# GpSimd joins the halves of w1's pieces for their sums, in place of TensorE's identity products

## The chip, the cores and the metric

One core of a Trainium2 chip runs the whole program. The metric is the device time of one launch in microseconds (us), of which several runs are made; a profile of one execution is read beside it. TensorE (PE) multiplies, VectorE (DVE), ScalarE (ACT) and GpSimd (POOL) work on vectors, and SyncE (SP) issues all DMAs here.

## What is computed

The attention works in chunks of 64 tokens, a gated layer (d_ff 2048) follows, then a second layer with a softmax-weighted unit and a normalization (d_ff 1024). There are 4608 tokens of width 512.

```python
scores = scale * np.matmul(q_c, k_c.transpose(0, 1, 2, 4, 3))
...
out = np.matmul(attn, v_c)

h = x @ w_in
g = h * (1.0 / (1.0 + np.exp(-h)))
return (g @ w_out).astype(np.float32)

h = x @ w_in
...
solu = h * sm
...
return (ln @ w_out).astype(np.float32)
```

## The kernel before

Every operand of a product is held as two float16 halves, high and low (`split`, L107: ACT writes the high half, VectorE or GpSimd the low one), and a product is three matmuls: high by high, high by low, low by high. The tokens go in nine blocks of 512. In blocks 0 and 1 (`FAST = 2`) the products with w1 and w2 are plain: `h_group` (L357) makes one of 16 columns groups of h by 12 matmuls, `x_part` (L637) gathers g @ w2. From block 2 on both are done on quarters with seven products in place of eight, and for that the weights must be there as sums and differences of their quarters. These are made once, while blocks 1 and 2 run, are written to DRAM (`w1s`, `w2s`), and are read back through a ring of tiles (`Ring`, L447).

The weights arrive as 64-bit numbers. `dec_scale`, `dec_bits` and `dec_split` (L124 to L150) decode a piece: ACT scales (L129), VectorE shifts and joins bits (L136, L137, L139), then ACT and GpSimd, or for w4 ACT and VectorE, split it. The last pieces, w3 and w4, are decoded in block 1; from the 33rd piece on the intermediate `wy` lies in SBUF, before in a PSUM bank (`wp`). w3's low halves are GpSimd's (L114, `w3q`), w4's VectorE's (L115, `w4l`).

The sums of w1 are the place of the change. w1 has eight pairs of pieces: piece p holds the upper rows of two column groups p and p + 8. `w1_sums(p)` (L422) stands in the loop over f of block 1 at the steps of the table `W1F` (L66). It calls `sums` (L408), which stores three quarters as they are (L411) and calls `pe_sums` (L380). There the high and low halves of each quarter are added in PSUM by two products with an identity (L391, tile `wq`, two banks a piece), ACT copies two quarters out (L398, `y`), and VectorE makes four sums (L403 to L406). Then each of four results is split again (L110 on ACT, L114 on GpSimd, tile `ws`, three staging buffers `xb0` to `xb2`) and stored (L417).

Beside it in block 1 run four `m_h` (L658, at f = 5, 7, 9, 11): two banks of products with w3 (L664), and for each the chain `m_norm` (L740) over VectorE, ACT and GpSimd: maximum (L670), exponential (L764), product with the sum (L766), square (L772), power on GpSimd (L779), scaling (L782), split (L783, L784) and two transposing DMAs (L794). One buffer each for `e` and `u` makes the four chains follow each other. `m_out` (L807, at f = 13, 15 and behind the loop) needs the transposed `uT` and all of w4. All PSUM tiles come from one pool of eight banks (`ps1`, L77), so TensorE waits where a bank is still read.

The order on each engine is found by the Tile scheduler from the program's order and priorities; `w1_sums` stands under `tc.high_priority(offset=1)`.

```python
with tc.high_priority(offset=1):
    for p in range(8):
        if W1F[p] == f:
            w1_sums(p)
```

Of the kernel before, what the change touches and what calls it, by code (L numbers as in the profile page):

```python
# [8 lines left out]
F32 = mybir.dt.float32  # L9
F16 = mybir.dt.float16  # L10
I32 = mybir.dt.int32
AF = mybir.ActivationFunctionType
ALU = mybir.AluOpType
# [3 lines left out]
P = 128  # L17
# [9 lines left out]
K1 = F1 // P  # L27
# [19 lines left out]
def fused(ctx: ExitStack, tc: tile.TileContext, qkv, w1, w2, w3, w4, g_ln, out):  # L47
    nc = tc.nc
    V, A, G, T = nc.vector, nc.scalar, nc.gpsimd, nc.tensor
# [14 lines left out]
    MO = (0, 1, 2, 3)  # L64
    W3S = [0, 3]
    W1F = [3, 5, 7, 9, 11, 13, 14, 15]  # L66
    W2F = [3, 1, 7, 3]
    EXB = [6, 7, 10, 13, 14]
    PHA = [4, 5, 6, 7, 8, 10, 11, 15, 32, 33, 34, 35]
# [4 lines left out]
    one = ctx.enter_context(tc.tile_pool(name="one", bufs=1))  # L74
# [7 lines left out]
    w1t = [one.tile([P, 2, KD, P], F16, tag=f"w1_{f}", name=f"w1_{f}") for f in range(K1)]  # L82
    w2t = {}
    for d in range(KD):
        for f in range(4):
            if f % 2 == 0:
                tag = f"w2_{2 * d + f // 2}" if d < 3 else f"q{12 + f // 2}"
                y = one.tile([P, 2, 2, 4, P], F16, tag=tag, name="w2t")
                w2t[d, f], w2t[d, f + 1] = y[:, 0], y[:, 1]

    w1s = [dram.tile([7, P, 2, 2, 2, P], F16, name=f"w1s{i}") for i in range(4)]
# [15 lines left out]
    def split(dst_h, dst_l, src, scale, eng_h, eng_l):  # L107

        if eng_h is A:
            A.activation(dst_h, src, AF.Copy, scale=scale)  # L110
        else:
            V.tensor_scalar(out=dst_h, in0=src, scalar1=scale, scalar2=None, op0=ALU.mult)
        if eng_l is G and scale == 1.0:
            return G.tensor_tensor(out=dst_l, in0=src, in1=dst_h, op=ALU.subtract).ins  # L114
        return V.scalar_tensor_tensor(out=dst_l, in0=src, scalar=scale, in1=dst_h,  # L115
                                      op0=ALU.mult, op1=ALU.subtract).ins
# [202 lines left out]
    xb, xf = {}, {}  # L319
# [54 lines left out]
    def flat(a, keep):  # L374

        if len(a.shape) == keep + 1:
            return a
        return a.rearrange("p l a b -> p l (a b)" if keep == 2 else "p a b -> p (a b)")

    def pe_sums(ys, quads, y1122=None):  # L380

        ys, quads = ([flat(a, k) for a in v] for v, k in ((ys, 1), (quads, 2)))
        n = 512 // quads[0].shape[2]

        def whole(qs):
            ps = [bank([P, n, 512 // n], "wq") for _ in range(len(qs) // n)]
            out = []
            for i, a in enumerate(qs):
                o = ps[i // n][:, i % n]
                for l in range(2):  # L390
                    T.matmul(o, ident16, a[:, l], start=l == 0, stop=l == 1)  # L391
                out.append(o)
            return ps, out

        y11, y12, y21, y22 = ys
        ps, o = whole([quads[0], quads[3]])
        if n == 2:
            A.activation(y1122, ps[0], AF.Copy)  # L398
        else:
            A.activation(y11, o[0], AF.Copy)  # L400
            A.activation(y22, o[1], AF.Copy)
        _, (p21, p12) = whole([quads[2], quads[1]])
        V.tensor_tensor(out=y22, in0=p21, in1=y22, op=ALU.add)  # L403
        V.tensor_tensor(out=y21, in0=y11, in1=p21, op=ALU.subtract)
        V.tensor_tensor(out=y11, in0=y22, in1=y11, op=ALU.subtract)
        V.tensor_tensor(out=y12, in0=p12, in1=y11, op=ALU.subtract)  # L406

    def sums(quads, dst, ys, staging, y1122=None):  # L408
        with tc.issue_after(last[0]):
            for j, a in ((0, quads[0]), (4, quads[1]), (6, quads[3])):  # L410
                nc.sync.dma_start(out=dst(j), in_=a)  # L411
        pe_sums(ys, quads, y1122)
        y11, y12, y21, y22 = ys
        for y, j in ((y11, 1), (y22, 2), (y21, 3), (y12, 5)):
            z = staging()
            split(z[:, 0], z[:, 1], y, 1.0, A, G)
            nc.sync.dma_start(out=dst(j), in_=z)  # L417

    sn, last = [0], [None]
    UL = V  # L420

    def w1_sums(p):  # L422
        wa, wb = w1t[p], w1t[p + K1 // 2]
        y = one.tile([P, 4, 2, P], F32, tag=f"q{10 + p % 2}", name="y")

        def staging():
            sn[0] += 1
            return one.tile([P, 2, 2, P], F16, tag=f"xb{sn[0] % 3}", name="ws")

        sums((wa[:, :, 0:2], wa[:, :, 2:4], wb[:, :, 0:2], wb[:, :, 2:4]),  # L430
             lambda j: w1s[p // 2][j, :, p % 2], [y[:, i] for i in range(4)], staging,
             y[:, 0::3].rearrange("p n a b -> p n (a b)"))

    def w2_sums(c, q):
        ys = [one.tile([P, 2, 4, P], F32, tag=f"q{10 + i}", name="y") for i in range(2)]
# [44 lines left out]
    def bank(shape, name):  # L480
        return ps1.tile(shape, F32, tag="mm", name=name)
# [361 lines left out]
    for k in range(KD):  # L843
        for n in range(2):
            y = w3q[n, k // 2]
# [43 lines left out]
    def weights(n=1):  # L889
        for _ in range(n):  # L890
            d3()
            d1()
            d2()
# [36 lines left out]
    for b in range(NB):  # L930
        m = b * TPB + TPB
        more = b + 1 < NB
        if FAST <= b:
            q_alloc(b)
        for f in range(K1):
            if b < FAST:
                if b == 1 and f in MHF:
                    n = MHF.index(f)
                    run(m_h(b - 1, MO[n], "m1", ("m2", ("h4", "h5"), ("h6", "h7"), ("h2", "h3"))[n]))
                if b == 1 and f in MOF:  # L940
                    run(m_out(b - 1, MO[MOF.index(f)]))
                h_group(b, f)
                if b == 0:
                    weights(NW0[f])
                    if f:
                        g_split(b, f - 1, GH)
                else:
                    y = g_split(b, f, A)
                    with tc.high_priority(offset=-50):
                        weights(NW1[f])  # L950
                    with tc.high_priority(offset=1):
                        for p in range(8):
                            if W1F[p] == f:
                                w1_sums(p)
                    if f == QF:
                        load_qk(m, ("q8",))
                        prep_qk(m, ahead=False)
            elif f % 8 == 0:
                if f and more:
                    load_qk(m, ("w1_14", "w1_15"))  # L960
                    prep_qk(m, ahead=False)
                if b == FAST:
                    for n in range(2):
                        run(m_h(b - 1, MO[f // 4 + n], *(("m1", "m2"), ("w2_5", "w2_4"))[n % 2]))
                if f and b == FAST:
                    for n in range(2):
                        run(m_out(b - 1, MO[n]))
                elif b > FAST:
                    run(m_fast(b - 1, 1) if f else begun, in_turn(*(m_out(b - 1, MO[n]) for n in range(2) if f)))
                run(h_fast(b, f // 4), h_fast(b, f // 4 + 1))  # L970
        if b == 0:
            g_split(b, K1 - 1, GH)
        else:
            run(m_out(b - 1, MO[TPB - 2], low=more))
        if b == FAST - 1:
            ring.load()
        def step(s):

            if not more:
                return  # L980
            if s == 0:
                if b < FAST - 1:
                    load_qk(m)
                    prep_qk(m)
                else:
                    load_qk(after(m))
                prep_v(m)
            if b and s == 1:
                run(m_out(b - 1, MO[TPB - 1]))
            AT_P = (3, 4, 6, 7) if b == 0 else (3, 4, 5, 6)  # L990
            if s in AT_S:
                i = AT_S.index(s)
                n = m + ORDER[i]
                a_scores(n)
                if i < 3:
                    prep_qk(m + ORDER[i + 1], V if b == 1 else G)
                a_norm(n, eng_l=V if b else G)
            if s in AT_P:
                i = AT_P.index(s)
                a_pv(m + ORDER[i])  # L1000
            if b == 0:
                with tc.high_priority(offset=-50):
                    weights(NX[s])
            if b == FAST and s in W3S:
                w3_sums(W3S.index(s))
            if b == 1:
                weights(NX1[s])
            for n in range(4):
                if b == 1 and W2F[n] == s:
                    w2_sums(n // 2, n % 2)  # L1010

        if b < FAST:
            for s in range(8):
                step(s)
                x_part(b, s // 2, s % 2)
        else:
            begun = m_fast(b, 0, alt=not more)
            x_fast(b, step, begun)

    b = NB - 1  # L1020
# [52 lines left out]
```

## Time and profile before

| | us |
|---|---|
| runs of the kernel, median of 3 | 1179.76 |
| lowest, highest run | 1178.94, 1181.08 |
| profiled execution, first to last instruction | 1179.4 |
| TensorE busy in it | 1127.8 (96%) |
| VectorE busy | 911.7 (77%) |
| GpSimd busy | 249.1 (21%) |

The page gives no other time for the profiled execution than its span; it lies 0.4 us under the median of the runs. Matmuls are pipelined, so their durations overlap: the pace is read from one start to the next. The granted TensorE clock (PEclk) is a share of the full 2.4 GHz, 0.50 is 1.2 GHz. "Idle before" names what ended an engine's wait. Line numbers are those of the kernel before; in the changed kernel they are up to 18 higher.

### The profile page before, as it was taken

The page shows a single profiled execution, that of the slowest core. Times are in us where ns is not written, and L with a number is a line of the kernel's source. Part 1 is how long each engine was busy: PE and PEld are TensorE (multiplying, and loading weights), DVE is VectorE, ACT ScalarE, POOL GpSimd, SP SyncE. Part 2 cuts the span into 40 slices and gives each one's busy share as a digit, 9 for nine tenths or more (in the row PEclk, how much of TensorE's full clock was granted, in tenths as well). Part 3 has the DMA queues.
Part 4 walks back from the last instruction along what each step waited for, and adds up shares of the span by engine and source line. Part 5 has one row for each costly group of instructions (what it writes and reads, how often), then busy time and mean ns, then how long its engine had stood idle before and what let it go on. Part 6 is the DMA issues. An engine that isn't in the chain of part 4 may idle for free.

```text
span 1179.4 us, 23566 instructions
## 1 busy us (share of the span) xinstructions
PE 1127.8 (96%) x9036; PEld 769.1 (65%) x9036; DVE 911.7 (77%) x1638; ACT 802.8 (68%) x1475; POOL 249.1 (21%) x243
## 2 busy tenths in 40 slices
PE   5999998998999999999999999999999999999998
PEld 4444443444657875887678767876787677777853
DVE  5999998487578787888778877888689868886453
ACT  6886678676667777856785677568756876577253
POOL 3655433334101510021003100310031002100001
PEclk9999899999999999999999999999999999999999
DMA  7667488543536564776577657666776676665704
GB/s 259 225 190 206 155 233 268 165 135 112 139 113 203 165 189 133 204 204 202 143 192 213 196 151 188 204 198 155 182 211 198 161 180 197 179 161 137 210 21 116
DMA packets 205169, 209.18 MB, mean 177 GB/s; under 512 B 120192, under 2 KB 130432, under 8 KB 205056
## 3 DMA queue, kind: packets, MB, share of 16 engines
q1 hardware_dynamic: 205056, 207.68, 61.5%
q8 instruction: 70, 1.15, 0.4%
q14 instruction: 43, 0.35, 0.1%
HBM read 156.24 MB, written 24.12 MB: 153 GB/s over the span
## 4 chain that ended last, share of the span: by engine, by line
PE 59%; DVE 16%; ACT 10%; DMA 7%; issue 6%; POOL 2%; SPq 0%; ACTq 0%; POOLq 0%; DVEq 0%
PE o_ps L821 5%; PE o_ps L813 5%; PE o_ps L814 5%; PE pa L491 3%; PE pa L594 3%; PE pa L592 3%; PE pa L593 3%; PE pa L493 3%; PE pa L492 3%; DVE vbl L115 2%; PE pa L708 2%; PE pa L709 2%; PE pa L710 2%; PE pb L491 2%; PE pb L493 2%
## 5 line engine op out<-in xcount | busy, mean ns | idle before, releaser
L110 ACT ACTIVATE q<-hc 128x512 f16<-128x512 f32 x196 | 119.1, 624 | 41.4 <-DVE hc L579 16.4
L115 DVE SCALAR_TENSOR_TENSOR q<-hc,q 128x512 f16<-128x512 f32 x196 | 138.0, 719 | 6.9 <-ACT q L110 5.5
L114 POOL TENSOR_TENSOR qbl<-qk,qbh 64x512 f16<-64x512 f32 x54 | 71.0, 1314 | 266.2 <-ACT qbh L110 223.6
L593 PE MATMUL pa<-q,ring 128*128 128x256 f16 x448 | 122.1, 273 | 0.0
L592 PE MATMUL pa<-q,ring 128*128 128x256 f16 x448 | 122.1, 273 | 0.0
L594 PE MATMUL pa<-q,ring 128*128 128x256 f16 x448 | 122.1, 273 | 0.0
L813 PE MATMUL o_ps<-w4h,uT 128*128 128x512 f16 x288 | 109.1, 379 | 0.4 <-DVE e L766 0.4
L814 PE MATMUL o_ps<-w4l,uT 128*128 128x512 f16 x288 | 109.2, 379 | 0.0
L779 POOL TENSOR_TENSOR c<-c,mhalf 128x2 f32<-128x2 f32 (+1 forms) x22 | 14.1, 640 | 392.1 <-DVE c L778 382.2
L492 PEld LDWEIGHTS <-ring 128*128 128x128 f16 x784 | 77.0, 98 | 18.4 <-issue 7.9
L491 PEld LDWEIGHTS <-ring 128*128 128x128 f16 x784 | 77.0, 98 | 11.5 <-DMA ring<-w1s 0.8
L592 PEld LDWEIGHTS <-ring 128*128 128x128 f16 x784 | 76.7, 98 | 11.1
L593 PEld LDWEIGHTS <-ring 128*128 128x128 f16 x784 | 76.7, 98 | 11.0
L493 PEld LDWEIGHTS <-ring 128*128 128x128 f16 x784 | 77.0, 98 | 9.2
L594 PEld LDWEIGHTS <-ring 128*128 128x128 f16 x784 | 76.7, 98 | 8.9
L821 PE MATMUL o_ps<-w4h,uT 128*128 128x512 f16 x288 | 70.2, 379 | 0.0
L491 PE MATMUL pa<-x,ring 128*128 128x256 f16 x224 | 61.6, 275 | 6.7 <-ACT hc L513 4.3
L493 PE MATMUL pa<-x,ring 128*128 128x256 f16 x224 | 61.7, 275 | 0.0
L492 PE MATMUL pa<-x,ring 128*128 128x256 f16 x224 | 61.6, 275 | 0.0
L491 PE MATMUL pb<-x,ring 128*128 128x256 f16 x224 | 61.1, 273 | 0.6 <-DMA ring<-w1s 0.6
L592 PE MATMUL pb<-q,ring 128*128 128x256 f16 x224 | 61.1, 273 | 0.0
L593 PE MATMUL pb<-q,ring 128*128 128x256 f16 x224 | 61.1, 273 | 0.0
(277 smaller groups left out, 3486.4 us busy)
## 6 DMA issues: line engine op xcount, KB each, us to landing
ring<-w1s SPq DMA_DIRECT2D x196, 256.0 KB, 3.4
ring<-w2s SPq DMA_DIRECT2D x196, 256.0 KB, 3.8
wst<-w SPq DMA_DIRECT2D x48, 512.0 KB, 4.1
qk<-qkv SPq DMA_DIRECT2D x29, 512.0 KB, 3.8
vs<-qkv SPq DMA_DIRECT2D x36, 256.0 KB, 3.2
out<-o SPq DMA_DIRECT2D x36, 256.0 KB, 2.2
w1s<-ws SPq DMA_DIRECT2D x32, 128.0 KB, 2.1
w2s<-ws SPq DMA_DIRECT2D x16, 256.0 KB, 2.0
```

The lines of the kernel that those rows point to most:

```text
L110: A.activation(dst_h, src, AF.Copy, scale=scale)
L114: return G.tensor_tensor(out=dst_l, in0=src, in1=dst_h, op=ALU.subtract).ins
L115: return V.scalar_tensor_tensor(out=dst_l, in0=src, scalar=scale, in1=dst_h, op0=ALU.mult, op1=ALU.subtract).ins
L491: T.matmul(ps[:, c], wh, x[:, 0, k], start=first, stop=False, skip_group_check=True)
L492: T.matmul(ps[:, c], wh, x[:, 1, k], start=False, stop=False, skip_group_check=True)
L493: T.matmul(ps[:, c], wl, x[:, 0, k], start=False, stop=k == 1, skip_group_check=True)
L592: T.matmul(ps[:, c], wh, g[:, 0], start=first, stop=False, skip_group_check=True)
L593: T.matmul(ps[:, c], wh, g[:, 1], start=False, stop=False, skip_group_check=True)
L594: T.matmul(ps[:, c], wl, g[:, 0], start=False, stop=q == 1 and f == 3, skip_group_check=True)
L813: T.matmul(ps, uh[:, k], w4h[:, k, :], start=k == 0, stop=False)
L814: T.matmul(ps, uh[:, k], w4l[:, k, :], start=False, stop=False)
L821: T.matmul(ps, ul[:, k], w4h[:, k, :], start=False, stop=k == K2 - 1)
```

## The change

The halves of each w1 piece are no longer added by identity products. A new function `join` adds them on GpSimd, two instructions of 512 elements a piece, into the tile `y` that the sums use (`w1_join`, at steps of a new table `W1J`). The sums (`quad_sums`) read only that tile. The four results are then split two at a time: two ACT and two GpSimd instructions of 512 in place of four each of 256, in a staging tile twice as large, from which the same four stores are made.

```diff
+    W1J = [1, 3, 5, 7, 9, 11, 13, 14]
...
-    def pe_sums(ys, quads, y1122=None):
+    def pe_sums(ys, quads):
...
-        if n == 2:
-            A.activation(y1122, ps[0], AF.Copy)
-        else:
-            A.activation(y11, o[0], AF.Copy)
-            A.activation(y22, o[1], AF.Copy)
+        A.activation(y11, o[0], AF.Copy)
+        A.activation(y22, o[1], AF.Copy)
...
+    def quad_sums(ys):
+        y11, y12, y21, y22 = ys
+        V.tensor_tensor(out=y22, in0=y21, in1=y22, op=ALU.add)
+        V.tensor_tensor(out=y21, in0=y11, in1=y21, op=ALU.subtract)
+        V.tensor_tensor(out=y11, in0=y22, in1=y11, op=ALU.subtract)
+        V.tensor_tensor(out=y12, in0=y12, in1=y11, op=ALU.subtract)
+
+    def join(y, w):
+        G.tensor_tensor(out=y, in0=flat(w[:, 0], 1), in1=flat(w[:, 1], 1), op=ALU.add)
...
+    def w1_join(p):
+        y1[p] = y = one.tile([P, 4, 2 * P], F32, tag=f"q{10 + p % 2}", name="y")
+        for i in range(2):
+            join(y[:, 2 * i:2 * i + 2].rearrange("p n a -> p (n a)"), w1t[p + i * K1 // 2])
+
     def w1_sums(p):
         wa, wb = w1t[p], w1t[p + K1 // 2]
-        y = one.tile([P, 4, 2, P], F32, tag=f"q{10 + p % 2}", name="y")
-
-        def staging():
+        y = y1.pop(p)
+        dst = lambda j: w1s[p // 2][j, :, p % 2].rearrange("p l a b -> p l (a b)")
+        with tc.issue_after(last[0]):
+            for j, a in ((0, wa[:, :, 0:2]), (4, wa[:, :, 2:4]), (6, wb[:, :, 2:4])):
+                nc.sync.dma_start(out=w1s[p // 2][j, :, p % 2], in_=a)
+        quad_sums([y[:, i] for i in range(4)])
+        for i, js in ((0, (1, 5)), (2, (3, 2))):
             sn[0] += 1
-            return one.tile([P, 2, 2, P], F16, tag=f"xb{sn[0] % 3}", name="ws")
-
-        sums((wa[:, :, 0:2], wa[:, :, 2:4], wb[:, :, 0:2], wb[:, :, 2:4]),
-             lambda j: w1s[p // 2][j, :, p % 2], [y[:, i] for i in range(4)], staging,
-             y[:, 0::3].rearrange("p n a b -> p n (a b)"))
+            z = one.tile([P, 2, 2, 2 * P], F16, tag=f"xb{sn[0] % 3}", name="ws")
+            split(z[:, 0], z[:, 1], y[:, i:i + 2], 1.0, A, G)
+            for k in range(2):
+                nc.sync.dma_start(out=dst(js[k]), in_=z[:, :, k])
...
                             if W1F[p] == f:
                                 w1_sums(p)
+                            if W1J[p] == f:
+                                w1_join(p)
```

The scheduler puts the work in another order. GpSimd's queue from the splits of w3 on, before (`w3q` is w3, `ws` a staging tile of sums, `c` the power of an m_norm):

```order
L114 TENSOR_TENSOR w3q<-wy,w3q 128x512 x8
L114 TENSOR_TENSOR ws<-y,ws 128x256 x4
L779 TENSOR_TENSOR c<-c,mhalf 128x1
L114 TENSOR_TENSOR ws<-y,ws 128x256 x5
L779 TENSOR_TENSOR c<-c,mhalf 128x1
```

and changed (`y<-w` is a join):

```order
L115 TENSOR_TENSOR w3q<-wy,w3q 128x512 x2
L414 TENSOR_TENSOR y<-w_0_72 128x512
L414 TENSOR_TENSOR y<-w_8_80 128x512
L115 TENSOR_TENSOR w3q<-wy,w3q 128x512
L414 TENSOR_TENSOR y<-w_1_73 128x512
L414 TENSOR_TENSOR y<-w_9_81 128x512
L115 TENSOR_TENSOR w3q<-wy,w3q 128x512
L115 TENSOR_TENSOR ws<-y,ws 128x512 x2
L414 TENSOR_TENSOR y<-w_2_74 128x512
L115 TENSOR_TENSOR w3q<-wy,w3q 128x512
```

Joins and splits of the first pieces now stand among the eight splits of w3; six joins and four `ws` splits come before or between them and the last one.

VectorE's queue from the end of m_norm 1 (`u_1931`) to the second product of m_norm 2 (`e_2072`), before; `y_2129` is piece 3 of w1, `w4l` the last piece of w4:

```order
L784 TENSOR_TENSOR u_1931<-e_1925,u_1931 128x1024
L672 TENSOR_REDUCE mm__2076<-mp_2073 128x1
L115 SCALAR_TENSOR_TENSOR w4l_109<-wy_2041,gs_110,w4h_108 128x512
L761 TENSOR_SCALAR nm_2079<-mm__2076 128x1
L115 SCALAR_TENSOR_TENSOR g_2036<-g_2120,g_2036 128x512
L403 TENSOR_TENSOR y_2129<-wq_2139,y_2129 128x256
L404 TENSOR_TENSOR y_2129<-y_2129,wq_2139 128x256
L405 TENSOR_TENSOR y_2129<-y_2129 128x256
L406 TENSOR_TENSOR y_2129<-wq_2139,y_2129 128x256
L115 SCALAR_TENSOR_TENSOR g_2179<-g_2177,g_2179 128x512
L766 SCALAR_TENSOR_TENSOR e_2072,us_2086<-h2_ps_2046,u_2078 128x512
```

and the end of the same stretch changed (`y_2305` is piece 6, `y_2343` piece 7, `e_2030` m_norm 2's `e`, L784 the former L766):

```order
L408 TENSOR_TENSOR y_2305<-y_2305 128x256
L116 SCALAR_TENSOR_TENSOR w4l_109<-wy_1999,gs_110,w4h_108 128x512
L409 TENSOR_TENSOR y_2305<-y_2305 128x256
L408 TENSOR_TENSOR y_2343<-y_2343 128x256
L410 TENSOR_TENSOR y_2305<-y_2305 128x256
L409 TENSOR_TENSOR y_2343<-y_2343 128x256
L411 TENSOR_TENSOR y_2305<-y_2305 128x256
L784 SCALAR_TENSOR_TENSOR e_2030,us_2044<-h2_ps_2004,u_2036 128x512
```

The sums have moved up by three to four pieces: where those of piece 3 stood, those of pieces 6 and 7 stand, and the last `w4l`, which stood two rows behind the end of m_norm 1 (counted from 0), has a sum of piece 6 ahead of it.

## Rows read from the trace of the kernel before

**Rows 1.** The page, busy us, share of the span and instructions by engine.

```profile
PE 1127.8 (96%) x9036; PEld 769.1 (65%) x9036; DVE 911.7 (77%) x1638; ACT 802.8 (68%) x1475; POOL 249.1 (21%) x243
```

**Rows 2.** Busy time by stretch: PE, PEld, DVE, ACT, POOL, then PEclk, DMA, GB/s.

```profile
131.20:160.00 28.80, 28.80 (x143) 13.89 (x142) 28.23 (x43) 20.20 (x35) 9.54 (x8) 1.00 0.57 171
160.00:197.00 37.00, 30.51 (x149) 14.37 (x148) 33.94 (x70) 32.25 (x59) 14.71 (x15) 1.00 0.92 264
197.00:225.00 28.00, 27.57 (x160) 13.88 (x159) 16.75 (x44) 19.97 (x39) 8.53 (x13) 1.00 0.63 195
...
236.00:242.00 6.00, 4.43 (x34) 2.59 (x35) 3.70 (x7) 4.03 (x7) 0.35 (x1) 0.72 0.38 112
```

**Rows 3.** TensorE's waits from 131 to 242: total us, times, longest.

```profile
PE wq L391 <- DVE e L766: 2.9, 1, 2.9
PE h_ps L362 <- DVE y L406: 2.1, 1, 2.1
PE s_ps L211 <- ACT kb L110: 1.4, 1, 1.4
...
PE s_ps L212 <- DVE kb L115: 0.6, 1, 0.6
```

**Rows 4.** Timeline of VectorE, 180 to 210: start, us, line, operation, out<-in.

```profile
180.50 0.68 DVE L766 SCALAR_TENSOR_TENSOR e<-h_ps,u 128x512 f32<-128x512 f32 x1
...
188.12 1.69 DVE L784 TENSOR_TENSOR u<-e,u 128x1024 f16<-128x1024 f32 x1
...
197.24 0.68 DVE L766 SCALAR_TENSOR_TENSOR e<-h_ps,u 128x512 f32<-128x512 f32 x1
...
209.56 0.68 DVE L766 SCALAR_TENSOR_TENSOR e<-h_ps,u 128x512 f32<-128x512 f32 x1
```

**Rows 5.** Timeline of TensorE, first identity products.

```profile
141.55 0.71 PE L391 MATMUL wq<-w,ident 128*128 128x256 f16 x5
142.10 0.38 PE L362 MATMUL h_ps<-x,w 128*128 128x512 f16 x1
```

**Rows 6.** Timelines of TensorE (first m_h, x-part's start) and GpSimd (last w3 split).

```profile
145.02 5.34 PE L664 MATMUL h_ps<-w3q,x 128*128 128x512 f16 x24
...
225.04 0.38 PE L645 MATMUL x_ps<-g,w2t 128*128 128x512 f16 x1
...
145.44 1.20 POOL L114 TENSOR_TENSOR w3q<-wy,w3q 128x512 f16<-128x512 f32 x1 [1.30 <-ACT w3q L110]
```

**Rows 7.** Timeline of VectorE, first two sums of piece 0.

```profile
152.36 0.42 DVE L403 TENSOR_TENSOR y<-wq,y 128x256 f32<-128x256 f32 x1
152.69 0.41 DVE L404 TENSOR_TENSOR y<-y,wq 128x256 f32<-128x256 f32 x1
```

**Rows 8.** Group of GpSimd, 120 to 242: busy us, mean ns, idle before.

```profile
L114 POOL TENSOR_TENSOR w3q<-wy,w3q 128x512 f16<-128x512 f32 x8 | 10.3, 1288 | 15.2 <-ACT w3q L110 15.2
```

**Rows 9.** Timelines of VectorE and GpSimd, 125.8 to 131.

```profile
125.82 0.42 DVE L136 TENSOR_SCALAR wy<-wy 128x512 int32<-128x512 int32 x1
...
127.00 1.53 DVE L139 SCALAR_TENSOR_TENSOR wy<-wst,wy 128x512 int32<-128x512 int32 x1
...
129.79 0.68 DVE L115 SCALAR_TENSOR_TENSOR x<-x_ps,x 128x512 f16<-128x512 f32 x1
...
126.65 1.33 POOL L114 TENSOR_TENSOR w3q<-wy,w3q 128x512 f16<-128x512 f32 x1 [2.02 <-ACT w3q L110]
```

**Rows 10.** Instructions on the tile wst: duration ns min/median/max, first and last start.

```profile
L137 DVE SCALAR_TENSOR_TENSOR wp<-wst,wp x32: 679/686/697, 14.2 to 115.8; 128x512 int32<-128x512 int32 x32
...
L137 DVE SCALAR_TENSOR_TENSOR wy<-wst,wy x16: 674/692/1651, 116.8 to 182.0; 128x512 int32<-128x512 int32 x16
```

**Rows 11.** Timeline of ACT, the wait of a split of the last piece.

```profile
235.19 0.42 ACT L110 ACTIVATE ws<-y 128x256 f16<-128x256 f32 x1 [2.14 <-DMA w1s<-ws]
```

**Rows 12.** SyncE's queue, fourth m_norm's transposes; the chain's piece for such a one.

```profile
215.22 2.58 SPq L794 DMA_TRANSPOSE uT<-u  x2
...
174.85 2.74 DMA uT<-u
```

More of the change, by code (lines that the diff above doesn't have):

```diff
@@ L406, in pe_sums, with sums @@
         V.tensor_tensor(out=y12, in0=p12, in1=y11, op=ALU.subtract)
-    def sums(quads, dst, ys, staging, y1122=None):
+    def quad_sums(ys):
[6 more added lines that the diff above has]
+        G.tensor_tensor(out=y, in0=flat(w[:, 0], 1), in1=flat(w[:, 1], 1), op=ALU.add)
+    def sums(quads, dst, ys, staging):
         with tc.issue_after(last[0]):
@@ L411, in sums @@
                 nc.sync.dma_start(out=dst(j), in_=a)
-        pe_sums(ys, quads, y1122)
+        pe_sums(ys, quads)
         y11, y12, y21, y22 = ys
@@ L420, in fused @@
     UL = V
+    y1 = {}
+    def w1_join(p):
+        y1[p] = y = one.tile([P, 4, 2 * P], F32, tag=f"q{10 + p % 2}", name="y")
+        for i in range(2):
+            join(y[:, 2 * i:2 * i + 2].rearrange("p n a -> p (n a)"), w1t[p + i * K1 // 2])
     def w1_sums(p):
         wa, wb = w1t[p], w1t[p + K1 // 2]
-        y = one.tile([P, 4, 2, P], F32, tag=f"q{10 + p % 2}", name="y")
-        def staging():
+        y = y1.pop(p)
[5 more added lines that the diff above has]
+        for i, js in ((0, (1, 5)), (2, (3, 2))):
             sn[0] += 1
-            return one.tile([P, 2, 2, P], F16, tag=f"xb{sn[0] % 3}", name="ws")
-        sums((wa[:, :, 0:2], wa[:, :, 2:4], wb[:, :, 0:2], wb[:, :, 2:4]),
-             lambda j: w1s[p // 2][j, :, p % 2], [y[:, i] for i in range(4)], staging,
-             y[:, 0::3].rearrange("p n a b -> p n (a b)"))
+            z = one.tile([P, 2, 2, 2 * P], F16, tag=f"xb{sn[0] % 3}", name="ws")
+            split(z[:, 0], z[:, 1], y[:, i:i + 2], 1.0, A, G)
+            for k in range(2):
+                nc.sync.dma_start(out=dst(js[k]), in_=z[:, :, k])
     def w2_sums(c, q):
```

## The prediction

> **What bounds the kernel now.** I read the page first: TensorE is busy 96% of a span of 1179.4 us, VectorE 77% [rows 1]. So what TensorE waits for sets the time, and a matmul less is worth something only where no wait takes its place. The second view is the table of stretches [rows 2]. Block 1's products with w1, in which the change lies, run from 131.2 to 225.0. The reader is to see two regimes: until 160 TensorE is full and VectorE nearly so (28.2 of 28.8); from 160 to 197 TensorE is busy 30.5 of 37 while VectorE is at 33.9; from 197 on TensorE is full again and VectorE has slack. The third view, TensorE's waits from 131 to 242, names the releasers: VectorE's L766, which frees the two banks of an m_norm, for 2.9, and the last sum of a w1 piece (L406) for 2.1 [rows 3]. So this stage is bounded by TensorE and VectorE in turn, and VectorE holds the chain m_norm by m_norm (0 to 3): L766 of m_norm 1 ends at 181.2, of 2 at 197.9, of 3 at 210.2 [rows 4].
>
> **What goes from TensorE.** Per piece eight identity products, 64 in all. Five take 0.55 us (141.55 to 142.10) [rows 5], so one takes 0.11 and all take 7.0 us. Their eight ACT copies (L398) and 16 banks go too. That is a gain only if TensorE isn't then waiting for VectorE.
>
> **What the banks now ask.** In the built program the banks freed by the sums go to the h and h2 tiles. With e1, e2, e3 for these three ends, m_h 3 needs a bank that e1 frees, h_group(14) one that e2 frees, and the x-part one that e3 frees. TensorE's work behind them: an m_h is 24 matmuls in 5.2 us [rows 6], an h_group 12 in 2.6, an m_out 24 in 5.2, the scores 0.7. After e2 stand two h_groups, two m_outs and the scores, 16.3 us; the x-part starts no sooner than e2 + 16.3, and no sooner than e1 + 34.5 (an m_h, three h_groups and an m_out more). Today it starts at 225.0 [rows 6]. With nothing delayed on VectorE it could start at 215.7, so the question is how late e2 gets.
>
> **What VectorE and GpSimd pay.** Count up to X, the end of m_norm 1's last VectorE work (L784, 189.8 today) [rows 4], from the end of the x split (L115) at 130.5 [rows 9].
> (a) Eleven more sums stand ahead of X (23 for 12), at 0.33 apiece (L403 at 152.36, L404 at 152.69 [rows 7]): 3.6. The decode of w4's last piece falls behind X: L137 and L139 at 0.69 [rows 10] and L136 at 0.42 [rows 9], a little less as they overlap, 1.7. Net +1.9.
> (b) The first sum now stands ahead of the last x split, and waits for the two joins of piece 0; h_group(0) needs that split. The joins can start when the third w3 piece has been decoded and take 2 x 1.2; this is about 1.0.
> (c) The joins. No row shows a join; the nearest are GpSimd's w3q splits, 128x512 with two inputs, 1288 ns [rows 8]. 16 joins and 16 splits of that size are 41 us where 32 splits of 256 stood, in a stage of some 100, so GpSimd itself has room. But see what a GpSimd instruction does to VectorE: with w3q on GpSimd from 126.65 to 127.98, VectorE's L139 beside it took 1.53 in place of 0.69 and ended 0.55 after GpSimd [rows 9]. L137 with its operand in PSUM (wp) never took over 697 ns in 32; with it in SBUF (wy) it took up to 1651 [rows 10]. Eight such stretched instructions beside the eight w3q splits lose 0.84 each by this row. About a seventh of VectorE's work up to X reads PSUM (the reduces, L766, an x2 split) and is not held, so I take 0.70 per 512-wide GpSimd instruction and 0.35 per half-wide one. Ahead of X stood 5 w3q and 13 half splits, 8.1 us; now 12 joins, 9 splits and 6 w3q, 18.9. That is +10.8.
> The sums were held little before, since three of the four read a PSUM bank; now all four read SBUF alone.
> X comes 1.9 + 1.0 + 10.8 = 13.7 later, at 203.5. Bounds: a GpSimd instruction costs VectorE nothing (X +2.9), or its whole 1.29: the 27 now count for 15.5 more than the 5 and 13 halves did, so +2.9 + 20.0 = +22.9.
>
> The Trainium skill, "SBUF — State Buffer", section "SBUF: two separate sides", gives the rule behind (c): a VectorE instruction in a two-port mode or with two SBUF inputs and a GpSimd instruction exclude each other, and whichever starts first holds the port pair for the whole instruction. Rows 9 and 10 agree in which instructions are held; in the price they show 0.84 where a whole instruction would be 1.33, since L139 began 0.35 after GpSimd and was done 0.55 after it. By the rows the sum is the one below; by the rule's whole instruction it is that of the second rival.
>
> (d) L766 of m_norm 2 now stands behind the first sum of piece 7, so behind that piece's join. From X on GpSimd has two joins of piece 6, three splits of w1, two of q and then the two joins: some eight ahead of the sum, 8 x 1.29 = 10.3, then 2.3 of sums and L766: e2 = X + 12.6. Today it is 197.9 - 189.8 = 8.1. That adds 4.5, and e2 comes 18.2 later, at 216.1.
> (e) So the x-part starts at 216.1 + 16.3 = 232.4 in place of 225.0: **+7.4**. The chain by e1 gives less, since about 10 later it is 191 + 34.5 = 226; m_out(0)'s last w4 piece also, as it needs X + 6 (209 less 3 for the seven pieces ahead of it, and 24 behind: 230).
> (f) w3: the last split ended at 146.64 and m_h began at 145.02 with that piece as its last quarter (from 149) [rows 6]. With six joins and four splits among the eight w3q this piece is some 6 later, so m_h waits about 3. It is covered: TensorE has to wait for e2 later anyway. Gone, it would cost those 3.
> (g) The tail: ACT's split of piece 7 waits 2.14 for its staging buffer at 235.19 and holds up the next qbh and kb [rows 11]; TensorE stands 2.0 (1.4 + 0.6) [rows 3], then runs from 236 to 242 at a clock of 0.72, more than half of it at 1.2 GHz in place of 2.4, which costs 6 x 0.28 = 1.7 [rows 2]. The sums are done long before that now: **-3.7**.
> (h) The fourth uT: today e3 to the last transpose issued and landed is 210.2 to 217.8 + 2.7 = 10.3 [rows 12]. Now e3 = 216.1 + 12.3 = 228.4 and uT is there at 238.7, while TensorE asks at 232.4 + 5.2 = 237.6: **+1.1**.
> SyncE: the 32 stores of sums read two pieces of 512 B where they read one of 1 KB; they move ahead with the sums, behind them queue the last loads of wst. These wait for decode already, so nothing. ACT loses eight copies and 16 of 32 splits' fixed part, off the path. The seven later blocks are untouched and shift as a whole.
> **Sum**: 7.4 - 3.7 + 1.1 = +4.8 on the span of 1179.4: 1184.2. The median of runs is 0.4 over the profiled span, so 1184.6.
>
> **Rivals.**
> - *The joins are nearly free.* VectorE has 3 of 37 us open from 160 to 197, and if GpSimd slips into its gaps X moves by 3 to 6. Then e2 is 205 to 208 and the x-part starts at 221.5 to 224.5, or at 218.6 (e1 + 34.5, with e1 2.9 late) if the wait in (d) doesn't come. With the tail that is 3 to 10 less than before: about 1174. Place: the bank that e2 frees. It decides at X +8.9 (x-part at 227.6, which the tail gives back), which is a price of 0.39 per GpSimd instruction. For it: beside an instruction with a PSUM operand GpSimd costs nothing [rows 10]. Against: 0.84 in rows 9, in a stretch as full as this one.
> - *Whole instructions are lost.* If VectorE always has an instruction waiting that both need, each GpSimd instruction costs it the full 1.29 [rows 8]. X +22.9, e2 +27.4, x-part at 241.6: +16.6 - 3.7 + 1.1 = +14, 1194. For it: 24 of the 32 sums come newly under it, since they read SBUF alone. Against: rows 9. This is the section of "SBUF — State Buffer" in the Trainium skill taken at its word.
> - *It comes to nothing:* the chain of m_norms, with its own waits, takes as long as now, gains at banks and tail cancel: 1180. That the change doesn't do what it says is out, since the order shows 64 products gone and 16 joins there.
>
> **How the numbers follow.** The forecast, slower by 3 to 8 (own range 1181 to 1189), has 0.5; joins nearly free 0.34; whole instructions lost 0.1; nothing 0.06. About 0.2%, 2.4 us, is what a measurement of this kernel tells from no change. Faster by over that (below 1177.4): 0.35. Within: the nothing case and the edges of the two sides, 0.13. Slower: 0.52. The range leaves out a tenth on each side: 1171 (near the best of the first rival) to 1194.
>
> **What would show it.** Right: 64 fewer matmuls and TensorE's busy time down by some 7; DVE L137 and L139 on wy more often over 1.3 us; joins at about 1.2 to 1.4 us; m_norm 2's L766 ending near 216 and the x-part beginning near 232; TensorE idle for longer between 160 and 215, the releaser VectorE's L766; no stall at 235. Wrong: L766 of m_norm 2 ending before 206, or joins well under 1 us, would mean that GpSimd took only VectorE's gaps; a wait of m_h on w3q of over 5 us would mean that GpSimd's queue and not the port set the pace.

## The result, and the profile after

The changed kernel takes **1191.21 us** (median of 4 runs, 1190.46 to 1192.35) against 1180.42 for the kernel before beside it: ratio 1.0096, 95% interval 1.0081 to 1.011. It is slower, as forecast, but by 10.8 where 4.8 was forecast. The profiled execution has a span of 1188.5, 9.1 over that of before.

The page's busy line of the changed kernel answers to [rows 1]:

```profile
PE 1126.2 (95%) x8972; PEld 763.7 (64%) x8972; DVE 929.0 (78%) x1638; ACT 797.1 (67%) x1451; POOL 274.2 (23%) x243
```

64 matmuls are gone (9036 to 8972), but TensorE's busy time fell by 1.6 only. VectorE has as many instructions as before and is busy 17.3 longer. The table by stretch shows both, against [rows 2] (same columns):

```profile
131.20:160.00 28.80, 22.25 (x85) 9.12 (x85) 26.86 (x35) 15.54 (x26) 22.83 (x15) 0.81 0.34 99
160.00:197.00 37.00, 30.32 (x121) 12.57 (x120) 35.29 (x60) 24.79 (x40) 16.52 (x12) 0.87 0.76 215
197.00:225.00 28.00, 23.67 (x94) 9.97 (x94) 27.12 (x51) 17.48 (x29) 18.09 (x13) 0.88 0.71 188
...
236.00:242.00 6.00, 6.00 (x51) 3.09 (x49) 3.44 (x11) 5.92 (x10) 0.55 (x1) 1.00 0.53 203
```

From 197 to 225 VectorE was open for 11 us; now it is full (27.12 of 28). TensorE, which stood full in the first and third stretch, is not in any, and the granted clock is 0.81 to 0.88: part of the time at 1.2 GHz in place of 2.4. TensorE's waits from 131.2 to 242 (total, times, longest):

```profile
PE h_ps L682 <- DVE e L784: 6.7, 2, 3.9
PE h_ps L682 <- ACT w3q L111: 3.5, 1, 3.5
PE h_ps L364 <- DVE x L116: 3.4, 1, 3.4
PE o_ps L832 <- DVE w4l L116: 2.3, 1, 2.3
PE o_ps L831 <- ACT w4h L111: 1.9, 1, 1.9
PE h_ps L682 <- POOL w3q L115: 0.6, 1, 0.6
```

L784 is the old L766, L682 the products of m_h. 18.4 us in all, where the same stretch of the kernel before has 8.7: twice for the bank that an m_norm frees, and for both w3 and w4, whose decode has become late. No `s_ps` wait is left [rows 3]. The last wait ahead of the x-part is for w4's last low half; behind it TensorE runs without one for 22.5 us (its timeline):

```profile
158.21 1.44 PE L682 MATMUL h_ps<-w3q,x 128*128 128x512 f16 x3 [0.64 <-POOL w3q L115]
180.56 8.34 PE L682 MATMUL h_ps<-w3q,x 128*128 128x512 f16 x24 [3.88 <-DVE e L784]
216.48 0.38 PE L832 MATMUL o_ps<-w4l,uT 128*128 128x512 f16 x1 [2.32 <-DVE w4l L116]
238.94 0.38 PE L663 MATMUL x_ps<-g,w2t 128*128 128x512 f16 x1
```

The first row is the end of m_h 0, at 159.65. VectorE comes to its maximum only 14.1 later:

```profile
173.78 1.27 DVE L688 TENSOR_REDUCE mp<-h_ps 128x1 f32<-128x512 f32 x2
```

So up to 216 it is VectorE, idle for some 4 us since 131.2, that sets the pace. Where its time went stands in its groups from 120 to 242 (busy us, mean ns, then the idle time before), and GpSimd's:

```profile
L137 DVE TENSOR_SCALAR wy<-wy 128x512 int32<-128x512 int32 x15 | 11.8, 789 | 2.1 <-ACT wy L130 2.1
L408 DVE TENSOR_TENSOR y<-y 128x256 f32<-128x256 f32 x8 | 7.1, 892 | 0.0
L411 DVE TENSOR_TENSOR y<-y 128x256 f32<-128x256 f32 x8 | 6.2, 776 | 0.0
L409 DVE TENSOR_TENSOR y<-y 128x256 f32<-128x256 f32 x8 | 5.2, 653 | 0.0
L410 DVE TENSOR_TENSOR y<-y 128x256 f32<-128x256 f32 x8 | 4.3, 533 | 0.0
L414 POOL TENSOR_TENSOR y<-w 128x512 f32<-128x512 f16 x16 | 23.4, 1480 | 2.6 <-DVE wy L140 2.2
L115 POOL TENSOR_TENSOR w3q<-wy,w3q 128x512 f16<-128x512 f32 x8 | 14.5, 1818 | 7.6 <-ACT w3q L111 7.6
```

The four sums are the same arithmetic as before, 0.41 each when nothing is in the way [rows 7]; now they take 0.53 to 0.89 on average, 22.8 us in all where the same window of the kernel before has 13.9. They never wait for a join (idle 0.0): the time lies inside the instruction. VectorE's timeline around the end of m_norm 1 (L802, 1.21 when free) and m_norm 2's products shows two durations and nothing between:

```profile
204.48 2.17 DVE L802 TENSOR_TENSOR u<-e,u 128x1024 f16<-128x1024 f32 x1
...
214.79 1.64 DVE L116 SCALAR_TENSOR_TENSOR w4l<-wy,gs,w4h 128x512 f16<-128x512 f32 x1
216.35 1.37 DVE L409 TENSOR_TENSOR y<-y 128x256 f32<-128x256 f32 x1
217.65 1.37 DVE L408 TENSOR_TENSOR y<-y 128x256 f32<-128x256 f32 x1
218.94 0.41 DVE L410 TENSOR_TENSOR y<-y 128x256 f32<-128x256 f32 x1
...
220.62 0.68 DVE L784 SCALAR_TENSOR_TENSOR e<-h_ps,u 128x512 f32<-128x512 f32 x1
```

2.17 - 1.21, 1.64 - 0.68 and 1.37 - 0.41 are all 0.96. GpSimd beside them:

```profile
204.09 3.58 POOL L414 TENSOR_TENSOR y<-w 128x512 f32<-128x512 f16 x2
...
214.67 2.77 POOL L414 TENSOR_TENSOR y<-w 128x512 f32<-128x512 f16 x2
217.41 1.33 POOL L115 TENSOR_TENSOR kb<-qk,kb 128x512 f16<-128x512 f32 x1
220.81 2.27 POOL L115 TENSOR_TENSOR ws<-y,ws 128x512 f16<-128x512 f32 x2 [2.08 <-ACT ws L111]
```

While GpSimd works without a gap (214.67 to 218.74) VectorE gets one such instruction done per GpSimd instruction, each 0.96 longer; when it stops, VectorE is back at 0.41.

### The profile page after: what moved, and what is told of

It reads as the page before. It is cut to its first block, busy times and chain, and to the rows that moved or that the text cites. A ratio compares the mean times of both kernels' runs of the same rounds, so it can differ in the third digit from the quotient of the medians.

```text
span 1188.5 us, 23370 instructions
## 1 busy us (share of the span) xinstructions
PE 1126.2 (95%) x8972; PEld 763.7 (64%) x8972; DVE 929.0 (78%) x1638; ACT 797.1 (67%) x1451; POOL 274.2 (23%) x243
## 3 DMA queue, kind: packets, MB, share of 16 engines
q8 instruction: 70, 1.15, 0.4%
## 4 chain that ended last, share of the span: by engine, by line
PE 62%; DVE 14%; ACT 10%; DMA 5%; issue 5%; POOL 3%; SPq 0%; ACTq 0%; POOLq 0%; DVEq 0%
PE o_ps L839 5%; PE o_ps L832 5%; PE o_ps L831 5%; PE pa L509 3%; PE pa L610 3%; PE pa L612 3%; PE pa L611 3%; PE pa L511 3%; PE pa L510 3%; DVE vbl L116 2%; PE pa L728 2%; PE pa L727 2%; PE pa L726 2%; PE pb L511 2%; PE pb L510 2%
## 5 line engine op out<-in xcount | busy, mean ns | idle before, releaser
L610 PE MATMUL pb<-q,ring 128*128 128x256 f16 x224 | 61.1, 273 | 0.0
L509 PE MATMUL pa<-xb,ring 128*128 128x256 f16 x224 | 61.1, 273 | 0.0
L510 PE MATMUL pa<-xb,ring 128*128 128x256 f16 x224 | 61.1, 273 | 0.0
```

What stands on the lines that cost most here:

```text
L509: T.matmul(ps[:, c], wh, x[:, 0, k], start=first, stop=False, skip_group_check=True)
L510: T.matmul(ps[:, c], wh, x[:, 1, k], start=False, stop=False, skip_group_check=True)
L610: T.matmul(ps[:, c], wh, g[:, 0], start=first, stop=False, skip_group_check=True)
```

## The experiments

Three theories at the start. **A**: a GpSimd instruction keeps VectorE's instructions on SBUF waiting inside, so VectorE reaches the end of each m_norm late. **B**: the joins delay GpSimd's own queue, the splits of w3 above all (the last began at 156.59 in place of 145.44), and what follows waits for that. **C**: the joins are innocent, the early sums and the paired splits do it. Twelve kernels were run. The table has the median of 4 to 12 runs, the ratio to the kernel before measured beside it (1180.4 to 1181.0) with its interval, and from each profile VectorE's busy time, the start of w3's last split, the end of m_norm 2's second product (the prediction's e2) and the start of block 2's first product.

| kernel | us | ratio | VectorE | w3 | e2 | block 2 |
|---|---|---|---|---|---|---|
| before | 1180.42 | 1 | 911.7 | 145.4 | 197.9 | 303.8 |
| after | 1191.21 | 1.0096 (1.0081 to 1.011) | 929.0 | 156.6 | 221.3 | 313.4 |
| run 1: no joins | 1177.73 | 0.9973 (0.9962 to 0.9985) | 914.0 | 152.7 | 207.6 | 300.5 |
| run 2: joins on VectorE | 1180.18 | 0.9989 (0.9976 to 1.0002) | 924.8 | 154.3 | 204.2 | 304.0 |
| run 3: joins behind w3 | 1186.27 | 1.0038 (1.0027 to 1.0049) | 926.2 | 146.4 | 215.8 | 310.8 |
| run 4: paired splits alone | 1181.65 | 1.0001 (0.9989 to 1.0012) | 909.5 | 146.8 | 201.0 | 304.4 |
| run 5: later, GpSimd | 1186.47 | 1.0049 (1.0032 to 1.0066) | 918.8 | 147.0 | 206.2 | 312.1 |
| run 6: later, VectorE | 1180.22 | 0.9993 (0.9983 to 1.0003) | 922.9 | 145.4 | 202.0 | 304.1 |
| run 7: decode in PSUM | 1178.39 | 0.9981 (0.997 to 0.9993) | 912.9 | 148.1 | 208.8 | 301.2 |
| run 8: the same, before | 1190.93 | 1.0083 (1.0065 to 1.0101) | 907.3 | 143.0 | 201.4 | 313.3 |
| run 9: as 7, no joins | 1166.87 | 0.9889 (0.9873 to 0.9904) | 911.2 | 147.2 | 199.6 | 291.6 |
| run 10: as 7, joins on VectorE | 1180.72 | 1.0006 (0.9997 to 1.0015) | 921.3 | 147.2 | 208.5 | 303.3 |
| run 11: as 7, joins behind w3 | 1176.42 | 0.9962 (0.9948 to 0.9976) | 915.3 | 143.3 | 201.8 | 300.2 |
| run 12: w3 alone in PSUM | 1186.36 | 1.0044 (1.003 to 1.0059) | 921.8 | 148.7 | 207.6 | 308.4 |

**Run 1, the joins left out.**

```diff
-        for i in range(2):
-            join(y[:, 2 * i:2 * i + 2].rearrange("p n a -> p (n a)"), w1t[p + i * K1 // 2])
...
-        quad_sums([y[:, i] for i in range(4)])
+        V.tensor_tensor(out=y[:, 3], in0=h21, in1=h22, op=ALU.add)
+        V.tensor_tensor(out=y[:, 2], in0=h11, in1=h21, op=ALU.subtract)
+        V.tensor_tensor(out=y[:, 0], in0=y[:, 3], in1=h11, op=ALU.subtract)
+        V.tensor_tensor(out=y[:, 1], in0=h12, in1=y[:, 0], op=ALU.subtract)
```

> The sixteen joins are left out and the four sums read the high halves of w1 alone, so the low halves of w1 are missing from the sums; the paired splits and everything else stay as in the changed kernel. Theory A (a GpSimd instruction of 512 holds VectorE's instructions that read SBUF, about 0.7 us for each, and VectorE sets when banks come free): VectorE's busy time falls by 8 to 17 us, m_norm 2's last product ends 10 to 15 earlier than 221.3, the x-part starts at 218 to 226, total 1175 to 1180. Theory B (what costs is GpSimd's own queue: six joins and four splits ahead of w3's last split, which came at 156.6 for 145.4 before): the last split of w3 comes near 148 and the total is 1172 to 1178 even if VectorE's busy time falls by less than 5. Theory C (the joins are innocent, the early sums and paired splits on VectorE and ACT do it): no change, 1188 to 1192.

13.5 us faster than the changed kernel, and faster than the kernel before. C falls: all sums stand as early as in the changed kernel and do no harm. VectorE's busy time is 15.0 lower, so a join costs VectorE 15.0 / 16 = **0.94**, though VectorE runs nothing of the join. A's other signs came too: e2 13.7 earlier, the x-part at 223.81. w3's last split still begins at 152.69, so B's condition (near 148) wasn't met.

**Run 2, the joins on VectorE** (`G.tensor_tensor` in `join` becomes `V.tensor_tensor`).

> The joins run on VectorE in place of GpSimd, 16 x about 0.65 = 10.4 us of VectorE's own work. Theory A (port): VectorE gains back what it lost by being held, 16 x 0.7 to 1.1 = 11 to 17, and pays 10.4, so m_norm 2's last product ends within 5 us of 221.3 and the total is 1186 to 1192. Theory B (GpSimd's queue): w3's last split comes near 148 in place of 156.6, m_norm 0 begins some 8 to 10 us earlier than 173.8 and the total is 1178 to 1184.

11.0 faster than the changed kernel. VectorE does sixteen instructions more and is busy 4.2 less. A was right that it gains more than it pays, wrong that this comes to nothing: m_norm 2's product ends 17 earlier, not within 5. Part of that is order: with the joins in VectorE's queue the scheduler places the sums of pieces 5 to 7 behind m_norm 2's product, so this run does not price the engine alone. B had the total right (1178 to 1184) with its condition unmet (154.34).

**Run 3, all joins behind w3's last split.**

```diff
-            split(wh, wl, yf, 1.0, A, G)
+            w3_last[0] = split(wh, wl, yf, 1.0, A, G)
...
+        with tc.issue_after(w3_last[0]):
+            for i in range(2):
+                join(y[:, 2 * i:2 * i + 2].rearrange("p n a -> p (n a)"), w1t[p + i * K1 // 2])
```

> All sixteen joins are ordered behind the last split of w3 on GpSimd; the work of every engine is that of the changed kernel. Theory A (port): the same sixteen joins still stand ahead of m_norm 2 or 3 and hold VectorE as often, so the total moves by under 3: 1187 to 1192. Theory B (queue): w3's last split comes at 146 to 149, m_h 0 no longer waits for it, m_norm 0's maximum comes near 161 to 165 in place of 173.8, and of the 13.9 us by which the x-part starts later at least 8 are gone: 1178 to 1184.

4.9 faster. w3 is on time, m_norm 0's maximum begins at 165.86 for 173.78, but e2 still ends at 215.8, and TensorE waits twice as long for the m_norms (its waits from 125 to 262; GpSimd's four joins behind the split are from its timeline):

```profile
PE h_ps L684 <- DVE e L786: 13.3, 2, 7.1
```

```profile
146.42 1.19 POOL L115 TENSOR_TENSOR w3q<-wy,w3q 128x512 f16<-128x512 f32 x1 [1.31 <-ACT w3q L111]
147.58 6.01 POOL L414 TENSOR_TENSOR y<-w 128x512 f32<-128x512 f16 x4
```

The order on VectorE moved with the joins (`W1J` also begins at 2 in place of 1): 7 sums stand ahead of m_norm 0's maximum in place of 15, and VectorE is busy 2.8 less. So the 4.9 is what joins and sums among the decodes of w3 cost; how much of it is w3's lateness by itself this run does not show. 1186.3 lies between B's range and A's, and 7.5 of the 13.9 at the x-part are gone where B asked for 8: each theory holds a part.

**Run 4, the paired splits alone** (the kernel before, its identity products kept, two splits of 512 for four of 256).

> The kernel before with the splits of the four results two at a time (two of 512 on ACT and on GpSimd in place of four of 256), the identity products kept. It prices the second half of the change alone. Theory A: 16 GpSimd instructions of 512 at 0.7 for 32 of 256 at 0.35 cost VectorE the same, so the total is that of before, 1178 to 1183. Rival: the pairing itself delays the stores (each waits for two results), total 1183 to 1188.

Nothing: 1.0001. In the kernel before, the second half of the change costs nothing and gives nothing.

**Runs 5 and 6, joins and sums moved behind the m_norms**, on GpSimd and on VectorE. `cs` and `uls` are the powers and the last instructions of the m_norms, `JA` and `SA` say behind which of them a piece's joins and sums are queued. These lines are run 5's; in run 6 joins and sums both follow `uls` by `SA = (0, 0, 1, 2, 2, 2, 3, 3)`, and their steps in `W1F` and `W1J` are later.

```diff
+    JA = (None, None, 0, 0, 1, 2, 2, 3)
+    SA = (None, None, 0, 1, 2, 3, 3, 3)
...
+        with tc.issue_after(w3_last[0] if JA[p] is None else cs[JA[p]]):
...
+        with after_(SA[p], uls):
+            quad_sums([y[:, i] for i in range(4)])
```

> Joins on GpSimd as in the changed kernel, all of them behind w3's last split and from the third piece on behind the powers of m_norms, and the sums of pieces 2 to 7 ordered behind the m_norms as in the kernel before (four pieces ahead of m_norm 2's last product in place of seven and a half). Theory A (each join ahead of these products holds VectorE 0.94 us, from the 15.0 us that VectorE's busy time lost when the sixteen joins were left out): some seven joins fewer stand ahead of m_norm 2's last product, 7 x 0.94 = 6.6 and 14 sums fewer, so it ends 6 to 11 earlier than the 215.8 of the run with the joins behind w3, and the total is 1176 to 1182. Theory B (only the joins ahead of w3's last split cost): as that run, 1184 to 1188.

> Joins on VectorE, joins and sums both behind the m_norms: none ahead of m_norm 0's products, two pieces ahead of m_norm 1's, three ahead of m_norm 2's. Theory A: VectorE is what paces 160 to 197, where two joins at 0.68 and four sums at 0.42 are 3.0 us a piece without a hold, and from 197 on it has 11 us open; m_norm 2's last product ends by 200, TensorE keeps the 7 us of identity products, total 1170 to 1177. Rival (the sums then come too late for the staging tiles and the first quarters of block 2, so what is won is lost at 235 to 305): 1178 to 1184.

Run 5 did to e2 what A said (206.2, 9.6 earlier than in run 3), and the total stayed. The waits of its TensorE from 125 to 262 show who took it:

```profile
PE h_ps L689 <- DVE e L791: 8.1, 2, 4.9
PE o_ps L838 <- ACT w4h L112: 4.9, 1, 4.9
...
PE s_ps L213 <- ACT kb L112: 2.2, 1, 2.2
PE s_ps L214 <- DVE kb L117: 1.9, 1, 1.9
```

The decode of w4 now ends the wait of m_out, and with the late sums a stall before the scores is back, 4.1 here and 2.0 in the kernel before [rows 3], which the change had removed. In run 6 the rival's total came, only in part by its reason: e2 is at 202.0, the scores wait 2.3, but m_out waits 6.4 for `w4l`, which neither side named. An earlier e2 alone bought nothing.

**Runs 7 and 8, the decode's intermediate in PSUM**, in the changed kernel and, as control, in the kernel before (`SB = 32` becomes `SB = 48`, so the last sixteen pieces decode through `wp`).

> The changed kernel with the intermediate of the last sixteen decodes in a PSUM bank in place of SBUF (two of VectorE's three decode instructions then have a PSUM operand in place of two SBUF operands); joins on GpSimd stay. Theory A (hold): VectorE's busy time falls by 8 to 14 from 929.0, the decodes at L138 and L140 take 0.69 each, total 1180 to 1187. Theory B (GpSimd's queue ahead of w3's last split): that split comes within 2 us of 156.6 and the total stays at 1188 to 1192.

> The kernel before with the same intermediate in PSUM, the control to the run above. Theory A: before, the two decode instructions lose (0.92 - 0.69) x 15 + (0.89 - 0.69) x 15 = 6.4 us to holds, so VectorE's busy time falls by 4 to 7 and the total is 1175 to 1180. Rival: a bank for each decode is missing for the identity products, 1181 to 1187.

In the changed kernel this gives back 12.8, with every join still on GpSimd, more than A's 4 to 11; VectorE's busy time fell by 16.1. Run 7's groups of VectorE (120 to 242):

```profile
L140 DVE SCALAR_TENSOR_TENSOR wy<-wst,wp 128x512 int32<-128x512 int32 x16 | 10.8, 677 | 1.0 <-POOL w3q L115 0.9
L138 DVE SCALAR_TENSOR_TENSOR wp<-wst,wp 128x512 int32<-128x512 int32 x15 | 10.1, 686 | 0.0
...
L408 DVE TENSOR_TENSOR y<-y 128x256 f32<-128x256 f32 x8 | 5.6, 698 | 6.2 <-POOL y L414 6.2
```

L138 took 1.11 on average in the changed kernel, L140 0.82; with a PSUM operand both are at 0.68, and GpSimd's w3 splits fell from 1.82 to 1.25. w3's last split is 8.5 earlier. That goes against B, for the six joins still stand ahead of it (and two `ws` splits for three). In the kernel before the same line costs 9.9, more than either side expected: TensorE waits 11.6 for L139, since a bank in decode is one that h lacks. In run 7 it waits 4.5 for the same (L140). That the identity products' banks, free since the change, make the difference fits this, but was not tried by itself.

**Runs 9 to 12: what the joins cost once the decode is out of the way.** Run 9 is run 1 with `SB = 48`, 10 is run 2, 11 is run 3 with it; 12 is the changed kernel with `SB = 40`.

> The intermediate of the last sixteen decodes in PSUM, and the sixteen joins left out (the sums read the high halves of w1 alone, so the low halves are missing from them). Beside the run with the joins and the decode in PSUM (1178.4, VectorE busy 912.9) it prices the joins where VectorE's decode is no longer held; without that the price was 13.5 on the total and 15.0 on VectorE. Theory A (the price is the hold on VectorE's instructions with two SBUF operands, most of them decode): 1 to 6 on the total, so 1172 to 1178, and 3 to 9 on VectorE's busy time. Theory B (the price is GpSimd's own queue): again some 13, so 1163 to 1168.

> The intermediate of the decodes in PSUM and the joins on VectorE. With the decode in SBUF this move from GpSimd to VectorE was worth 11. Theory A: with the hold mostly gone the joins are cheaper on GpSimd than 16 x 0.68 = 10.9 on VectorE, so the move is worth nothing or costs some: 1178 to 1184. Theory B: the move takes as much out of GpSimd's queue as before and is worth 5 or more: 1168 to 1174.

> The intermediate of the decodes in PSUM and all joins (on GpSimd) ordered behind w3's last split. With the decode in SBUF this order was worth 4.9. Theory A: w3's last split was late because VectorE's decode and GpSimd's work held each other, which the bank removes, so the order is worth under 2: 1176 to 1180. Theory B: the six joins ahead of it in the queue delay it by themselves, worth 4 to 6: 1172 to 1175.

> The changed kernel with the intermediate in PSUM for w3's eight pieces alone, w4's eight stay in SBUF. Theory A: about half of the 16.1 that VectorE's busy time fell by with all sixteen, so 918 to 924, and w3's last split near 150; the m_norms from 175 on are still held, total 1181 to 1187. Rival (the banks that w4's pieces took cost as much as the hold, TensorE waited 4.5 for L140 and 4.8 for L784 in that run): 1174 to 1179, which would be the best order of all.

Run 9 (the low halves missing, as in run 1) contradicts A on the total and lies in B's range: the joins still cost 11.5, though VectorE is busy only 1.7 longer with them. What is left is the 6.2 in the row above: L408, the first sum of a piece, now waits at the head of VectorE's queue for the join, up to 3.39 at once, with m_norm 2's products behind it (from run 7's timeline of VectorE):

```profile
203.69 1.36 DVE L408 TENSOR_TENSOR y<-y 128x256 f32<-128x256 f32 x1 [3.39 <-POOL y L414]
204.97 1.28 DVE L688 TENSOR_REDUCE mp<-h_ps 128x1 f32<-128x512 f32 x2
206.17 1.40 DVE L409 TENSOR_TENSOR y<-y 128x256 f32<-128x256 f32 x1
207.49 0.68 DVE L784 SCALAR_TENSOR_TENSOR e<-h_ps,u 128x512 f32<-128x512 f32 x1
```

6.2 + 1.7 = 7.9 of the 9.3 by which e2 ends later than in run 9. So B was right that GpSimd's queue matters, though not by w3 but by the sums. That this wait makes the whole of the 11.5 was not tried by itself and stays open. Run 10 went as A said (2.3 more than run 7), run 12 too, and run 11 at the edge (2.0 less where under 2 was expected). Run 11 is the best that computes everything: 4.0 under the kernel before, 14.8 under the changed one.

## Why the prediction was nearly right

The sign held, and so did the mechanism (held VectorE instructions, late banks) and the outer range, 1171 to 1194. The size did not: 1191.2 lies above the forecast's own range of 1181 to 1189 and nearer to the second rival's 1194 than to 1184.6.

- **TensorE, 7.0 of products gone.** They went, but not as time: TensorE waits 9.7 longer, and with five of its waits the clock fell to 1.2 GHz (granted 0.50 to 0.51), for 26.6 us between 131.2 and 225 in all, with TensorE busy in 21.5 of them; in the kernel before it is 1.00 there throughout. Half of the 21.5, some 11 us, is an estimate of the price; m_h 2's 24 products took 8.34 in place of 5.34 [rows 6]. Of the clock the prediction reckoned with the tail alone. Most of it did not lengthen the run, since VectorE came to m_h 2's products 11.5 after their end; behind the last wait, from 216.48, it cost some 1.7 (eight products took 3.17 for 1.89, two more 0.4).
- **(a)** The sums did move up. Run 1 has them as early and is faster than before, so this is not what cost.
- **(b) 1.0 forecast, 3.1 found.** The x split began at 132.90 in place of 129.79 [rows 9], behind L408, which itself took 1.37, and TensorE waited 3.4 for it.
- **(c) 0.70 per GpSimd instruction forecast.** Run 1 gives 0.94 per join, the timeline 0.96 for each held instruction. Up to X, the end of m_norm 1, VectorE's instructions take 22.6 longer than the shortest of their kind, and 9.8 before: 0.84 for each of the 27 that the prediction counts now, 0.85 for each of the 11.5 that it counts before. So the 0.84 of [rows 9] was the price; the seventh taken off it was wrong, and +12.8 belongs in place of +10.8. The bounds (0 and 1.29) hold it, and it lies above the 0.39 at which the first rival would have won. X was forecast at 203.5 and came at 206.65.
- **(d) and (e): here a step failed.** e2 was forecast at 216.1 and came at 221.3, 14.65 behind X where 12.6 was reckoned. But TensorE never waited for e2, which (e) makes the bound of the x-part; it came to that bank 1.4 after e2. Its last wait was for the last piece of w4, which (e) set aside as "X + 6": `w4l` ended at 216.43, X + 9.8, because six of VectorE's instructions on the way were held 0.9 to 0.97 each. The x-part began at 238.94 for 232.4. In run 3 TensorE does wait for e2 (1.8), and X (203.86), e2 (215.8) and the x-part (231.39) come out as forecast; but 19 sums stand ahead of X there in place of 23, so that agreement is in part luck.
- **(f)** w3's last split began 11.2 later where some 6 were forecast, with six joins and three `ws` splits ahead (four was a miscount), and m_h waited 4.1 for 3, under the 5 that would have spoken for GpSimd's queue. That m_h's wait would not count held, though not for the reason given: m_h 0's products then lay ready for 14.1 until VectorE came to them. What (f) lacks is the way back into VectorE: the decode waits for the buffer that a w3 split reads (last section).
- **(g) -3.7 forecast.** No stall at 235, the clock from 236 to 242 at 1.00 for 0.72. From the x-part to block 2 it took 74.4 for 78.7: **-4.3**. **(h) +1.1** did not come: no wait for `uT` in the rows.
- **The sum.** X was 3.2 short, X to e2 2.0, e2 to the x-part 1.3; (g) gave 0.6 more, (h) cost 1.1 less, and 0.5 was won behind the start of block 2. That is the 4.3 between +9.1 and +4.8 on the profiled span. Most of the rest lies in the 0.4 from span to run time: it compares two executions, and the profiled run of the changed kernel lies 2.0 over its own span (1190.46 for 1188.5).
- **Rivals.** *Nearly free* fell with the price of 0.94. *Whole instructions lost* came closer than its chance of 0.1 says: 0.96 of the 1.15 of the shortest join. The Trainium skill's rule ("SBUF — State Buffer", section "SBUF: two separate sides"), that the one that starts first has the shared ports for the whole instruction, agrees with the two durations in the timeline, but not with the stretch from 150.04 in the last section, where six VectorE instructions that began behind a GpSimd one went ahead of it.

## What to carry to other kernels

Work moved to an idle engine is priced by what it does to the full one beside it: look in the trace for one instruction with two durations, and count how many will be in the way. Where several waits compete for one point, reckon for each what stands ahead of it on the full engine, holds included: the one set aside can be the last. And a late product costs nothing while the full engine comes to it later still (here 14 us). When a change frees a resource (here PSUM banks), ask what else could use it: the decode in PSUM lost 10 before the change and won 13 behind it.

## What the runs showed that was not expected

VectorE keeps GpSimd out as well, and longer. GpSimd's timeline in the changed kernel:

```profile
146.30 1.33 POOL L115 TENSOR_TENSOR w3q<-wy,w3q 128x512 f16<-128x512 f32 x1
150.19 4.62 POOL L115 TENSOR_TENSOR w3q<-wy,w3q 128x512 f16<-128x512 f32 x1 [2.56 <-ACT w3q L111]
```

and VectorE's in the same stretch:

```profile
150.04 0.68 DVE L116 SCALAR_TENSOR_TENSOR vbl<-vs,vbh 64x512 f16<-64x512 f32 x1
...
153.12 0.68 DVE L140 SCALAR_TENSOR_TENSOR wy<-wst,wy 128x512 int32<-128x512 int32 x1
155.54 0.67 DVE L137 TENSOR_SCALAR wy<-wy 128x512 int32<-128x512 int32 x1 [1.74 <-ACT wy L130]
```

From 150.04 to 153.80 VectorE ran seven instructions on SBUF, each at its short duration, and one GpSimd split that began in that time took 4.62, until VectorE had run dry; the next decode waited 3.69 on ACT for that split's buffer. In run 1, without joins, one took 3.20. In the stretch from 214.67 the two took turns, one for one; what decides between the two patterns stays open. And L137, with a single SBUF operand (0.41 when free), was held too: 0.79 on average.
